# First pair of blocks: R, U, Y and the state product of block 3 half an item sooner, and three of Y's six small transfers issued by GpSimd

## The chip, the cores and the metric

The kernel runs on one core of one Trainium2 chip. The metric is device time in microseconds: the median of three runs, 589.41 us for the kernel before (589.01 to 589.84).

A core has five engines, each with its own queue of instructions that it works off in order: TensorE (PE, matmuls into PSUM; its weight loads are PEld), VectorE (DVE), ScalarE (ACT), GpSimd (POOL), and SyncE (SP), which here only issues transfers. They wait for each other through semaphores.

## The reference, cut to what matters

A delta-rule attention over 4 x 8 heads, 768 steps, head size 48, whose output is the input of a feed-forward layer (384 to 2048 to 384, 3072 tokens).

```python
def _attn_ref(q, k, v, beta):
    k_n = k / (np.linalg.norm(k, axis=-1, keepdims=True) + 1e-06)
    state = np.zeros((B, H, D, D), dtype=np.float32)
    for t in range(S):
        kt, vt, bt = (k_n[:, :, t], v[:, :, t], beta[:, :, t, None])
        y[:, :, t] = np.einsum('bhd,bhde->bhe', q[:, :, t], state)
        v_old = np.einsum('bhde,bhd->bhe', state, kt)
        state = state + bt[:, :, :, None] * np.einsum('bhd,bhe->bhde', kt, vt - v_old)

def _moe_ref(x, w_in, w_out):
    h = x @ w_in
    g = np.where(h >= 1, h, np.where(h <= -1, 0.0, (h + 1) ** 2 / 4))
    return g @ w_out
```

## The kernel before, in words

The 768 steps are cut into 12 blocks of 64 steps (block index `g`, 0 to 11), and two blocks make a pair (`G`, 0 to 5). Within a block the steps of a head are solved together: the Gram matrix of the keys (`gram_k`, L237) gives a triangular system, whose inverse is made on VectorE, all heads in lanes (transposes, norms, then 30 steps of `pr` and `A`, L366 and L368, and two closing transposes, L376 and L379), and put together by `merge` products. The state (tile `SU`) is then carried from block to block by a chain of four products on TensorE, each read out by ScalarE or VectorE before the next can start:

- R (`chain_r`, L492): the state times the keys, subtracted from the values by VectorE (L498);
- U (`chain_u`, L508): the inverse times these, copied to `SU` by ScalarE (L517);
- Y (`chain_y`, L534): the block's output, put into `xb` as a rounded part and a remainder (ScalarE L583 and L586, VectorE L590 and L592), and six small transfers of 32 KB (L595) that move the fourth head of each group to its rows of `xb`;
- the state product (`chain_d`, L607), added to the state by VectorE (L626).

The feed-forward layer runs beside that, as items: an item is a pair of blocks and one of 16 slices of the 2048 hidden units. Its up-projection (L738, nine matmuls into `h`) reads `xb`; ScalarE and VectorE turn `h` into `ghi` and `glo` (L877, L891, VectorE L893; then L856, VectorE L857), and two items later the down-projection (L753) adds into `o`. The first pair has 22 items: six for block 0 alone, ten for both, six for block 1 alone (256 columns wide). Items are numbered here from 0; item 22 is the first of the second pair, and its up-projection is the first that reads the Y of blocks 2 and 3.

The order of all engines is written out by hand. Each item has two places (2n and 2n+1) in two tables. `pe` holds products of the attention: those of place 2n stand on TensorE behind the item's up-projection, and are read out right after; those of place 2n+1 stand behind its down-projection, and are read out at the start of the next item. `fill` holds everything else: steps of the solve on VectorE and loads on SyncE; at a place 2n they are written down behind the read-out of that place's products. `at(table, G, t, ...)` puts something t items after the pair's first item. For the first pair M is 14, so `chain` starts 15.5 items in: U, Y and the state product of block 2 at the places 31, 32 and 34, then R, U, Y and the state product of block 3 (L784). `gram_k` of block 5 comes M + 3.5 items in, at place 35 (L832), the steps of the next solve (`lane_steps`, L833) at 32, 37, 38, 39 and 40: two are copies of the Gram matrices on ScalarE (L304), then come a transpose on VectorE with a root on ScalarE (L317, L281), eight short operations for norms and factors (L282 to L327), and the scaling of the system (L330), after which GpSimd masks it (L331) and the 30 steps can begin.

PSUM is shared: `h` has two buffers, so the up-projection of item n needs the L893 of item n-2; from item 12 on the attention's products have two buffers (`ch`) in all, so each of them also needs the read-out of the one before it. The keys and values of a coming block (`KV`) are loaded by SyncE in the order of `fill`, and scaled on VectorE (L292) between steps of the solve.

Of the kernel before, what the change touches and what calls it, by code (L numbers as in the profile page):

```python
# [7 lines left out]
F32 = mybir.dt.float32  # L8
# [5 lines left out]
C = 64  # L14
NP = 4
D = 48
# [24 lines left out]
def delta_rule_moe(ctx: ExitStack, tc: tile.TileContext, kqa, kqb, kv, beta, w, out):  # L41
# [14 lines left out]
    nc = tc.nc  # L56
# [4 lines left out]
    NB = CB * C  # L61
# [19 lines left out]
    def half(x):  # L81
        return slice(x * H, x * H + H)
# [80 lines left out]
    def dense(n):  # L163
        for _ in range(n):
            nc.tensor.matmul(warm_ps, warm[:, 0:P], warm, start=True, stop=True)  # L165
# [56 lines left out]
    def quarters():  # L222
        return [(e, x) for e in range(2) for x in range(2)]

    def banks(*shape):
        return [ps.tile([P, H, *shape], F32, **acc()) for _ in range(2)]
# [4 lines left out]
    def gram_k(g):  # L231

        x, b_ = KE.pop(g) if g in KE else K[g], banks(C)
        for j in range(H):
            for e, f in quarters():
                k, o = x[f * C:f * C + D, e * H + j, :], (1 - e) * C
                nc.tensor.matmul(b_[f][o:o + C, j], k, k, start=True, stop=True)  # L237

        def evict():
            for f in range(2):  # L240
                nc.scalar.copy(out=(GE[g - 2] if g in (2, 3) else GG[:, g % 2])[:, half(f)], in_=b_[f])
        return evict
# [158 lines left out]
    def merge16_a(g):  # L401
        y = ps.tile([P, NU, 16], F32, **acc())
        for u in range(NU):
            for r in QS:
                nc.tensor.matmul(y[r:r + 32, u], GG[r:r + 32, g, u, 32:64], XT[r:r + 32, g, u, 48:64], start=True, stop=True)

        def evict():
            if "Y" not in S:
                S["Y"] = own[:, NU * C:4 * DM].rearrange("p (g u t) -> p g u t", g=2, t=16)
            elif g == 0:  # L410
                S["Y"] = sb.tile([P, 2, NU, 16], F32, name="A16", bufs=1)
            nc.scalar.copy(out=S["Y"][:, g], in_=y)
        return evict
# [106 lines left out]
    def chain_y(g):  # L520
# [7 lines left out]
        xb = XB[g // 2]  # L528
# [14 lines left out]
        if g == 0:  # L543
            y0 = ps.tile([P, CT, NP, C], F32, **acc())
            for i in range(NT):
                for p in range(3):
                    for e in range(2):
                        for o in range(2):
                            r = o if (e, i) != (1, 1) else 1 - o
# [28 lines left out]
        def evict():  # L578
            parts = []
            for i in range(NT):  # L580
                hi, lo = (xb[:, x, :, g % 2 * NB:g % 2 * NB + NB].rearrange("p k (e s t) -> p s e k t", s=CT, t=C)[:, i] for x in range(2))
                shi, slo = (stg[:, x].rearrange("p (e s t) -> p s e t", s=CT, t=C)[:, i] for x in range(2))
                nc.scalar.copy(out=shi, in_=yy[i][:, :, 3])  # L583
                parts.append((yy[i], hi, lo, shi, slo))
            for y, hi, lo, shi, slo in parts:
                nc.scalar.copy(out=hi, in_=y[:, :, 0:3])  # L586

            def after():
                for y, hi, lo, shi, slo in parts:
                    nc.vector.tensor_tensor(out=slo, in0=y[:, :, 3], in1=shi, op=ALU.subtract)  # L590
                for y, hi, lo, shi, slo in parts:
                    nc.vector.tensor_tensor(out=lo, in0=y[:, :, 0:3], in1=hi, op=ALU.subtract)  # L592
                for k in range(3):
                    for r in (0, C):
                        (nc.gpsimd if g == 1 and r else nc.sync).dma_start(out=xb.bitcast(F32)[r + D:r + C, :, k, g % 2 * NB:g % 2 * NB + NB],  # L595
                                          in_=stg.bitcast(F32)[r + 16 * k:r + 16 * k + 16])
            return after
        return evict
# [175 lines left out]
    pe, fill = {}, {}  # L774

    def at(where, G, t, *x):
        where.setdefault(2 * first[G] + int(round(2 * t)), []).extend(x)
# [3 lines left out]
            at(fill, G, t + j, (gen, 1))  # L781

    def chain(G, t, a):
        for j, f, g in ((0, chain_u, a), (0.5, chain_y, a), (1.5, chain_d, a), (2.5, chain_r, a + 1), (3.5, chain_u, a + 1), (4, chain_y, a + 1), (5, chain_d, a + 1)):  # L784
            if (f, g) != (chain_d, ntot - 1):
                at(pe, G, t + j, lambda f=f, g=g: f(g))

    def plan(G):

        a, b = 2 * G + 2, 2 * G + 3  # L790
        if G == NS - 1:
            return
        if G == 0:
            made = dict(f=lambda n: dense(n) or (lambda: None), a=lambda g: merge16_a(g % 2), b=lambda g: merge16_b(g % 2), c=lambda g: merge32(g, None, True), e=lambda g: merge32(None, g), u=chain_u, y=chain_y, d=chain_d, r=chain_r, q=gram_q)
            for j, names in PIECES:
                for x in names.split():
                    at(pe, 0, j / 2, lambda f=made[x[0]], g=int(x[1]): f(g))
            M = MERGE / 2
            last = FT + HALF
        else:  # L800
            so, un = solves.pop(G)
            va, vb = scale_v(a), scale_v(b)
            at(fill, G, 0.5, (va, 1))
            at(fill, G, 1, (va, 1))
            at(pe, G, 2.5, lambda: chain_r(a))
            at(pe, G, 4.5, lambda: gram_q(a))
            at(pe, G, 6, lambda: gram_q(b))
            cost, hs = 0, 0
            t, n = (MERGE / 2 + 7 - FT - HALF, 30 + 2 * HALF - MERGE) if G == 1 else (-1, 15)
            for j in range(1, 31):  # L810
                at(fill, G, t + hs / 2, (so, 1))
                cost += j * (31 - j) + 150
                hs = int(cost / 9461 * n)
            for t in (6.5, 7, 7.5, 7.5, 7.5, 8.5):
                at(fill, G, t, (un, 1))
            at(fill, G, 9, (vb, 1))
            at(fill, G, 9.5, (vb, 1))
            M = 8.5
            last = 16
        if G:  # L820
            at(pe, G, 8, merge_first)
            at(pe, G, 9, merge_second)
        else:
            for j, x in ((0, (0, None)), (0.5, (1, 0)), (2.5, (None, 1))):
                at(pe, G, M + j, lambda x=x: merge32(*x))
        chain(G, M + 1.5, a)
        if G < NS - 2:
            if G:
                at(fill, G, 6.5, (load_k, a + 2))
            at(fill, G, M + 0.5, (load_k, b + 2, (nc.sync, nc.sync), True))  # L830
            at(pe, G, M + 1, lambda: gram_k(a + 2))
            at(pe, G, M + 3.5, lambda: gram_k(b + 2))  # L832
            lane_steps(G, M + 2, lanes(G + 2), 2.5, 3, 3.5, 4)  # L833
            solves[G + 1] = solve_whole(), unlanes_whole()
            at(fill, G, M + 3, (load_q, a + 2))
            at(fill, G, M + 5, (load_k, b + 2))
            at(fill, G, M + 6.5, (load_q, b + 2))
            at(fill, G, last + 0.5, (load_kv, a + 2))
            at(fill, G, last + 1.5, (load_kv, b + 2))

    solves = {}
    for G in range(NS):
        plan(G)
# [55 lines left out]
    G = NS - 1  # L899
# [50 lines left out]
```

## Time and profile before

| what | before |
|---|---|
| median of 3 runs | 589.41 us (589.01 to 589.84) |
| the profiled execution, and its span | 590.3 us, 588.6 us |
| TensorE busy | 569.0 us (97%), granted clock 0.992 in the mean |
| VectorE, ScalarE, GpSimd busy | 405.2 us (69%), 327.5 us (56%), 54.5 us (9%) |
| up-projections L738 | 918 matmuls, 223.0 us, mean 386 ns |
| down-projections L753 | 1152 matmuls, 329.4 us |
| small transfers L595 | 66 of 32 KB, median 2.0 us to landing |

The profile is of one execution; its times are counted from the start of its span. Rows of a timeline give the start, the busy time, engine, line, operation and tiles of one or of merged instructions, and in brackets how long the engine had stood idle before it and what ended that. The part that the change touches lies between 145 us and 210 us: items 16 to 21 of the first pair and the first items of the second.

### The profile page before, as it was taken

To read this page: it belongs to the slowest core of one execution; us is meant where nothing else is said; L and a number is where in the kernel's file an instruction comes from. 1 tells how busy PE (TensorE), PEld (TensorE's weight loads), DVE (VectorE), ACT (ScalarE), POOL (GpSimd) and SP (SyncE) were. 2 spreads that over 40 slices of the span, in tenths; PEclk is the share of its full clock that TensorE was granted. 3 is DMA by queue.
4 is the path that set the end of the run, shared out by engine and by line. 5 is a ranking of instruction groups with operands and counts; after the bars stand their busy time and mean duration, and the time that the engine had idled before them with its cause. 6 is when DMAs were issued, how large, how long until landed. Compare 5 with 4: busy or idle time off the path is not lost.

```text
span 588.6 us, 21697 instructions
## 1 busy us (share of the span) xinstructions
PE 569.0 (97%) x9585; PEld 493.3 (84%) x9585; DVE 405.2 (69%) x828; ACT 327.5 (56%) x587; POOL 54.5 (9%) x91
## 2 busy tenths in 40 slices
PE   8998899999999999999999999999999999999996
PEld 7776788788978888888888888888888888898986
DVE  5977999963689864599954599954599955333332
ACT  4648886358644575545575445575445564454443
POOL 6200010000000500010400011300011300000000
PEclk9979999999999999999999999999999999999999
DMA  5673766200333111134011134011133000020001
GB/s 147 199 253 138 213 212 192 77 4 10 95 81 100 31 32 39 39 97 114 24 33 41 37 103 119 16 30 45 36 106 96 1 3 16 15 55 1 0 2 53
DMA packets 32302, 42.77 MB, mean 73 GB/s; under 512 B 7056, under 2 KB 26768, under 8 KB 32208
## 3 DMA queue, kind: packets, MB, share of 16 engines
q1 hardware_dynamic: 31216, 40.41, 24.0%
q8 instruction: 75, 1.23, 0.9%
q0 software_dynamic: 576, 0.57, 0.4%
q10 hardware_dynamic: 416, 0.39, 0.2%
q14 instruction: 19, 0.16, 0.1%
HBM read 34.47 MB, written 4.72 MB: 67 GB/s over the span
## 4 chain that ended last, share of the span: by engine, by line
PE 47%; issue 22%; DVE 14%; DMA 6%; SPq 6%; ACT 2%; POOL 1%; POOLq 0%; DVEq 0%; ACTq 0%
PE h L738 18%; PE o L753 17%; DMA wt<-in_w_dram 4%; PE ch L534 3%; PE ch L237 2%; DVE s L893 2%; PE ch L508 2%; DVE pr L366 1%; DVE A L368 1%; DVE glo L857 1%; PE ch L250 1%; SPq L595 1%; PE ch L492 1%; DMA KV<-in_kv_dram 1%; DVE wt L208 1%
## 5 line engine op out<-in xcount | busy, mean ns | idle before, releaser
L738 PE MATMUL h<-xb,wt 128*128 128x512 f32 (+1 forms) x918 | 223.0, 386 | 5.1 <-DVE s L893 2.0
L753 PE MATMUL o<-wt,ghi 128*128 128x384 f32 x768 | 200.0, 342 | 0.1
L738 PEld LDWEIGHTS h<-xb,wt 128*128 128x128 f32 x918 | 161.8, 188 | 38.9 <-DVE s L893 3.4
L753 PEld LDWEIGHTS o<-wt,ghi 128*128 128x128 f32 x768 | 137.2, 188 | 7.0 <-issue 0.3
L753 PE MATMUL o<-wt,glo 128*128 128x384 f32 x384 | 129.4, 337 | 0.4 <-DVE glo L857 0.4
L856 ACT CAST ghi<-s 128x512 fp32r<-128x512 f32 (+1 forms) x102 | 60.8, 597 | 120.4 <-DVE s L893 107.8
L893 DVE SCALAR_TENSOR_TENSOR s<-s,h 128x512 f32<-128x512 f32 (+1 forms) x102 | 66.3, 650 | 77.1 <-ACT s L891 76.8
L877 ACT ACTIVATE s<-h,half 128x512 f32<-128x512 f32 (+1 forms) x102 | 67.4, 661 | 53.8 <-PE h L738 53.6
L857 DVE TENSOR_TENSOR glo<-s,ghi 128x512 fp32r<-128x512 f32 (+1 forms) x102 | 66.8, 654 | 39.5 <-ACT ghi L856 39.3
L753 PEld LDWEIGHTS o<-wt,glo 128*128 128x128 f32 x384 | 72.1, 188 | 1.0 <-DVE glo L857 1.0
L891 ACT ACTIVATE s<-s 128x512 f32<-128x512 f32 (+1 forms) x102 | 62.2, 610 | 2.2
L368 DVE TENSOR_TENSOR A<-A,pr 128x30 f32<-128x30 f32 (+14 forms) x120 | 45.4, 378 | 4.4
L366 DVE TENSOR_TENSOR pr<-A 128x30 f32<-128x30 f32 (+14 forms) x120 | 43.4, 362 | 2.2
L272 POOL TENSOR_SCALAR_AFFINE_SELECT Q<-Q 64x512 f32<-64x512 f32 x32 | 21.7, 680 | 117.4 <-ACT Q L260 116.0
L165 PE MATMUL o<-wx 128*128 128x512 f32 x87 | 27.8, 464 | 1.5 <-DVE tiny L175 1.5
L534 PEld LDWEIGHTS ch<-Q,SU 64*64 64x64 f32 (+3 forms) x1056 | 22.4, 135 | 3.7 <-ACT ghi L856 1.5
L534 PE MATMUL ch<-Q,SU 64*64 64x64 f32 (+3 forms) x1056 | 24.7, 222 | 0.0
L331 POOL TENSOR_SCALAR_AFFINE_SELECT A<-A 128x1024 f32<-128x1024 f32 x4 | 5.6, 1390 | 191.5 <-DMA xb<-X 148.1
L165 PEld LDWEIGHTS o<-wx 128*128 128x128 f32 x87 | 18.2, 220 | 5.6 <-DVE tiny L175 1.5
L626 DVE TENSOR_TENSOR SU<-ch,SU 48x384 f32<-48x384 f32 x36 | 19.9, 554 | 3.9 <-PE ch L607 3.5
L590 DVE TENSOR_TENSOR X<-ch,X 128x128 fp32r<-128x128 f32 x20 | 5.8, 292 | 23.5 <-ACT xb L586 22.5
L517 ACT COPY SU<-ch 64x384 f32<-64x384 f32 (+1 forms) x30 | 14.3, 476 | 7.0 <-PE ch L508 6.7
(168 smaller groups left out, 559.5 us busy)
## 6 DMA issues: line engine op xcount, KB each, us to landing
wt<-in_w_dram SPq DMA_DIRECT2D x16, 768.0 KB, 5.6
out_dram<-wx SPq DMA_DIRECT2D x44, 96.0 KB, 2.2
KV<-in_kv_dram SPq DMA_DIRECT2D x36, 96.0 KB, 2.4
KV<-in_kv_dram SPq DMA_DIRECT2D x72, 48.0 KB, 2.3
KV<-in_kv_dram SPq DMA_DIRECT2D x12, 192.0 KB, 2.7
xb<-X SPq DMA_DIRECT2D x60, 32.0 KB, 2.0
K<-in_kqb_dram SPq DMA_DIRECT2D x12, 128.0 KB, 2.6
Q<-in_kqb_dram SPq DMA_DIRECT2D x12, 128.0 KB, 2.7
```

The source lines that it names most:

```text
L165: nc.tensor.matmul(warm_ps, warm[:, 0:P], warm, start=True, stop=True)
L272: nc.gpsimd.affine_select(out=y, in_=y, pattern=[[0, H], [1, C]], base=0, channel_multiplier=-1, compare_op=ALU.is_gt, fill=0.0)
L366: nc.vector.tensor_tensor(out=pr, in0=A[:, 0:n, j:j + 1].broadcast_to([P, n, m]), in1=A[:, j:j + 1, j + 1:32].broadcast_to([P, n, m]), op= ...
L368: nc.vector.tensor_tensor(out=A[:, 0:n, j + 1:32], in0=A[:, 0:n, j + 1:32], in1=pr, op=ALU.add)
L534: nc.tensor.matmul(yy[i][o * C:o * C + C, e, p], SF[rows, u:u + C], w_[rows, x, k, :], **how)
L738: nc.tensor.matmul(h[:, cols(bs)], WT[f][:, 0, x, k * P:(k + 1) * P], XB[G][:, y, k, cols(bs)], start=(n == 0), stop=(n == 8))
L753: nc.tensor.matmul(oacc[G, k], (ghi, glo)[x][:, k * P:(k + 1) * P], WT[f][:, 1, y, :], start=(new and n == 0), stop=(left[G, b] == 0 and n ...
L856: nc.scalar.copy(out=ghi[:, c], in_=s[:, c])
L857: nc.vector.tensor_tensor(out=glo[:, c], in0=s[:, c], in1=ghi[:, c], op=ALU.subtract)
L877: nc.scalar.activation(out=s[:, c], in_=h[:, c], func=AF.Relu, bias=mid, scale=0.5)
L891: nc.scalar.activation(out=s[:, c], in_=s[:, c], func=AF.Square)
L893: nc.vector.scalar_tensor_tensor(out=s[:, c], in0=s[:, c], scalar=1.0, in1=h[:, c], op0=ALU.min, op1=ALU.max)
```

## The change

Three edits. For the first pair alone (`G` = 0), R, U, Y and the state product of block 3 move from 2.5, 3.5, 4 and 5 items behind the chain's start to 2, 3, 3.5 and 4.5, that is from the places 36, 38, 39 and 41 to 35, 37, 38 and 40. `gram_k` of block 5, at place 35 so far, moves to 36. And of the six small transfers of block 3's Y, the three for the upper 64 rows are issued by GpSimd, as those of block 1 are already.

```diff
                 for k in range(3):
                     for r in (0, C):
-                        (nc.gpsimd if g == 1 and r else nc.sync).dma_start(out=xb.bitcast(F32)[...],
+                        (nc.gpsimd if g in (1, 3) and r else nc.sync).dma_start(out=xb.bitcast(F32)[...],
...
     def chain(G, t, a):
-        for j, f, g in ((0, chain_u, a), (0.5, chain_y, a), (1.5, chain_d, a), (2.5, chain_r, a + 1), (3.5, chain_u, a + 1), (4, chain_y, a + 1), (5, chain_d, a + 1)):
+        for j, f, g in zip((0, 0.5, 1.5, 2.5, 3.5, 4, 5) if G else (0, 0.5, 1.5, 2, 3, 3.5, 4.5), (chain_u, chain_y, chain_d, chain_r, chain_u, chain_y, chain_d), (a, a, a, a + 1, a + 1, a + 1, a + 1)):
             if (f, g) != (chain_d, ntot - 1):
                 at(pe, G, t + j, lambda f=f, g=g: f(g))
...
             at(pe, G, M + 1, lambda: gram_k(a + 2))
-            at(pe, G, M + 3.5, lambda: gram_k(b + 2))
+            at(pe, G, M + (3.5 if G else 4), lambda: gram_k(b + 2))
```

On TensorE, between items 17 and 21, the difference of the two orders reads as follows (R is L492, the Gram product L237, U L508, Y L534, the state product L607, L738 an up-projection; the down-projections are left out).

```order
+L492 MATMUL ch<-SU,K 64x48 x32
+L738 MATMUL h<-xb,wt_1093 128x256 x9
 L237 MATMUL ch<-A 64x64 x32
-L738 MATMUL h<-xb,wt_1093 128x256 x9
-L492 MATMUL ch<-SU,K 64x48 x32
...
+L508 MATMUL ch<-KV,XT 64x48 x32
 L738 MATMUL h<-xb,wt_1106 128x256 x9
-L508 MATMUL ch<-KV,XT 64x48 x32
...
+L534 MATMUL ch<-Q,SU 64x64 x48
...
-L534 MATMUL ch<-Q,SU 64x64 x48
 L738 MATMUL h<-xb,wt_1205 128x256 x9
+L607 MATMUL ch<-SU,KV 48x48 x32
```

R stands where the Gram product stood, the Gram product behind the next up-projection, and U, Y and the state product each ahead of an up- or a down-projection that they stood behind.

On VectorE, from the `glo` of item 18 to the first step of the solve, the order before is this (`s_2880` belongs to item 19, `s_3029` to item 20; L592 writes Y, L626 the state).

```order
L857 TENSOR_TENSOR glo_2867<-s_2818,ghi_2866 128x256
L317 STREAM_TRANSPOSE A_2919<-GG_172 128x1024
L893 SCALAR_TENSOR_TENSOR s_2880<-s_2880,h_2870 128x256
L282 RECIPROCAL r1_2989<-y0_2988 128x32
...
L592 TENSOR_TENSOR xb_2567<-ch_2937,xb_2567 128x2x3x64
L857 TENSOR_TENSOR glo_3016<-s_2880,ghi_3015 128x256
L330 SCALAR_TENSOR_TENSOR A_2919<-A_2919,gm_2995 128x1024
L893 SCALAR_TENSOR_TENSOR s_3029<-s_3029,h_3019 128x256
L626 TENSOR_TENSOR SU_171<-ch_3041,SU_171 48x384 x2
L626 TENSOR_TENSOR SU_171<-ch_3042,SU_171 48x384 x2
L857 TENSOR_TENSOR glo_3088<-s_3029,ghi_3087 128x256
L366 TENSOR_TENSOR pr_3103<-A_2919 128x30
```

In the changed kernel the same stretch of VectorE reads as follows (`s_2917` is item 19's now).

```order
L857 TENSOR_TENSOR glo_2904<-s_2818,ghi_2903 128x256
...
L592 TENSOR_TENSOR xb_2567<-ch_2921,xb_2567 128x2x3x64
L317 STREAM_TRANSPOSE A_2984<-GG_172 128x1024
L893 SCALAR_TENSOR_TENSOR s_2917<-s_2917,h_2907 128x256
L282 RECIPROCAL r1_3003<-y0_3002 128x32
...
L857 TENSOR_TENSOR glo_3016<-s_2917,ghi_3015 128x256
L626 TENSOR_TENSOR SU_171<-ch_3031,SU_171 48x384 x2
L626 TENSOR_TENSOR SU_171<-ch_3032,SU_171 48x384 x2
L330 SCALAR_TENSOR_TENSOR A_2984<-A_2984,gm_3009 128x1024
L893 SCALAR_TENSOR_TENSOR s_3029<-s_3029,h_3019 128x256
L857 TENSOR_TENSOR glo_3088<-s_3029,ghi_3087 128x256
```

Y's read-out (L590 and L592) went from behind the transpose and the eight short operations to ahead of them, and the four additions to the state (L626) from behind the scaling L330 and item 20's L893 to ahead of both.

On SyncE, behind the output transfers of block 0, the difference begins as follows.

```order
-L93 DMA K<-in_kqb_dram 64x512
-L94 DMA K<-in_kqa_dram 48x512
...
-L595 DMA xb<-X 16x2x256 x6
+L595 DMA xb<-X 16x2x256 x3
+L93 DMA K<-in_kqb_dram 64x512
+L94 DMA K<-in_kqa_dram 48x512
...
 L102 DMA Q<-in_kqb_dram 64x512
```

Three of Y's transfers left SyncE, and the six key loads of block 5 moved from ahead of Y's transfers to behind them.

## Rows read from the trace of the kernel before

**Rows 1.** What TensorE waited for, from 206 us to the end.
```profile
PE ch L462 <- DVE XT L376: 0.4, 1, 0.4
PE h L738 <- DMA xb<-X: 0.2, 1, 0.2
```

**Rows 2.** The chain of waits, 145 to 210 us: start, us, what.
```profile
149.96 1.15 PE ch L237 x62
151.11 1.26 PE h L738 x9
152.37 1.08 PE ch L492 x64
153.45 1.25 PE o L753 x6
...
155.75 1.08 PE ch L508 x64
...
172.07 2.20 DMA KV<-in_kv_dram
...
206.28 1.40 PE ch L462 x82
```

**Rows 3.** Timeline of VectorE, 138 to 215 us.
```profile
155.72 2.02 DVE L317 STREAM_TRANSPOSE A<-GG 128x1024 f32<-128x1024 f32 x1
...
159.01 0.35 DVE L282 RECIPROCAL r<-y 128x32 f32<-128x32 f32 x1
...
160.81 0.20 DVE L327 STREAM_TRANSPOSE N<-N 128x32 f32<-128x32 f32 x1
...
161.72 1.01 DVE L592 TENSOR_TENSOR xb<-ch,xb 128x384 fp32r<-128x384 f32 x2
...
162.98 1.22 DVE L330 SCALAR_TENSOR_TENSOR A<-A,gm 128x1024 f32<-128x1024 f32 x1
...
164.45 2.25 DVE L626 TENSOR_TENSOR SU<-ch,SU 48x384 f32<-48x384 f32 x4
...
167.07 0.18 DVE L366 TENSOR_TENSOR pr<-A 128x30 f32<-128x30 f32 x1
...
174.39 0.56 DVE L292 TENSOR_TENSOR KV<-KV,N 128x384 f32<-128x384 f32 x1 [1.16 <-DMA KV<-in_kv_dram]
...
201.06 0.69 DVE L893 SCALAR_TENSOR_TENSOR s<-s,h 128x512 f32<-128x512 f32 x1 [1.51 <-ACT s L891]
```

**Rows 4.** Timeline of TensorE, 145 to 215 us: item 22's up-projection.
```profile
166.87 1.96 PE L738 MATMUL h<-xb,wt 128*128 128x512 f32 x6 [0.77 <-DVE SU L626]
```

**Rows 5.** Timeline of ScalarE, 138 to 215 us.
```profile
151.14 1.07 ACT L241 COPY GG<-ch 128x512 f32<-128x512 f32 x2 [1.78 <-PE ch L237]
...
153.25 1.23 ACT L304 COPY GG<-GG 32x512 f32<-32x512 f32 x2
...
156.86 1.46 ACT L517 COPY SU<-ch 64x384 f32<-64x384 f32 x3 [0.60 <-PE ch L508]
...
158.54 0.34 ACT L281 ACTIVATE y<-A,tiny 128x32 f32<-128x32 f32 x1
```

**Rows 6.** Timeline of GpSimd, 130 to 210 us.
```profile
164.50 1.26 POOL L331 TENSOR_SCALAR_AFFINE_SELECT A<-A 128x1024 f32<-128x1024 f32 x1 [43.45 <-PE ch L607]
```

**Rows 7.** Timeline of SyncE's queue, 140 to 200 us.
```profile
162.80 4.91 SPq L595 DMA_DIRECT2D xb<-X  x6
167.80 0.54 SPq L102 DMA_DIRECT2D Q<-in_kqb_dram  x1
...
170.87 0.52 SPq L113 DMA_DIRECT2D KV<-in_kv_dram  x1
```

**Rows 8.** Stretches: length, busy us (instructions) by engine, TensorE's clock, DMA share, GB/s.
```profile
27.00:30.00 3.00, 1.27 (x77) 0.86 (x65) 3.00 (x4) 1.49 (x3) 0.12 (x2) 1.00 0.41 99
30.00:37.00 7.00, 6.71 (x112) 5.27 (x112) 6.71 (x19) 1.59 (x3) 0.00 (x0) 0.51 0.98 368
46.00:48.20 2.20, 0.73 (x34) 0.58 (x30) 0.56 (x1) 0.99 (x2) 0.00 (x0) 1.00 0.99 406
```

More of the change, by code (lines that the diff above doesn't have):

```diff
@@ L594, in after @@
                     for r in (0, C):
-                        (nc.gpsimd if g == 1 and r else nc.sync).dma_start(out=xb.bitcast(F32)[r + D:r + C, :, k, g % 2 * NB:g % 2 * NB + NB],
+                        (nc.gpsimd if g in (1, 3) and r else nc.sync).dma_start(out=xb.bitcast(F32)[r + D:r + C, :, k, g % 2 * NB:g % 2 * NB + NB],
                                           in_=stg.bitcast(F32)[r + 16 * k:r + 16 * k + 16])
```

## The prediction

> **What bounds the kernel now.** I read the waits of TensorE first, and by stretch. From 206 us to the end it waits twice, for 0.4 and 0.2 us [rows 1]: there TensorE alone sets the time, and whatever delay it has at 206 us it keeps to the end. The first of these waits is the place to watch: L462, the merge product that needs the finished solve, waits 0.4 us for VectorE's closing transpose L376. So TensorE and VectorE reach 206 us almost together. The chain of waits, read next, shows by what way [rows 2]: through TensorE's products until Y, then through transfers to the values of the next block (the piece that starts at 172.07 and takes 2.20), and from there along VectorE to L462 at 206.28. The timeline of VectorE tells why [rows 3]: the solve's first step L366 starts at 167.07, L292 stands idle 1.16 us for the values, and then only one other wait is left, 1.51 us at 201.06. VectorE is the bound of the stretch from 167 to 206 us. TensorE's own stall, at item 22's up-projection (0.77 us at 166.87, where Y's transfers have to land) [rows 4], is not what decides: behind it TensorE would meet VectorE anyway.
>
> So the question to put to the change is when VectorE starts the 30 steps of the solve.
>
> **TensorE and ScalarE up to Y.** R takes the Gram product's slot. That slot's row starts at 149.96, when the four additions to the state have freed the PSUM buffers; R waits for the same additions. R takes 1.08: to 151.04. Item 18's up-projection 1.26: to 152.30. The Gram product, now behind it, 1.15: to 153.45. Its buffers must first be emptied of R by two VectorE subtractions of 128x384, which at the 0.56 of L292's row make 1.1 us and lie beside the 1.26; were that cover gone, some tenths would be lost. Then the down-projection 1.25, to 154.70, and U 1.08, to 155.78 [rows 2]. Before, U ended at 155.75 + 1.08 = 156.83, and its copies (L517) began at 156.86. So U itself comes 1.05 sooner. But on ScalarE the Gram copies (1.07, from 153.45), a square and the two L304 (1.23) now stand ahead of them [rows 5]: 153.45 + 1.07 + 1.23 = 155.75 without the square, and up to 156.2 with it. I take 156.0 for the start of L517, between U's end 155.8 and 156.2: 0.85 sooner than before.
>
> **Y.** Behind L517 nothing changes until Y is read out: before, L592 ended 162.73 - 156.86 = 5.87 after L517 began [rows 3, 5]. Now it ends at 156.0 + 5.9 = 161.9. The change asks for more than that in half an item, but U has to wait for the Gram copies.
>
> **VectorE behind Y.** This is the term that counts. Before, the transpose L317 and the eight short operations ran at 155.72 to 157.74 and 159.01 to 161.01, while VectorE had nothing else; they were done before Y's read-out. Now they are queued behind it on VectorE, and the additions to the state come ahead of L330. From 161.9:
> - L317, 2.02: to 163.9.
> - The root on ScalarE needs it: 0.34 [rows 5], to 164.3 with a hop to and fro. Item 19's L893 lies beside it.
> - L282 to L327, 161.01 - 159.01 = 2.00: to 166.3.
> - The `glo` of item 19 and four L626. Before, four L626 and one such `glo` filled 164.45 to 167.07, 2.62: to 168.9. Their input, the state product, is there by then (it needs only Y's read-out).
> - L330, 1.22: to 170.15.
> - GpSimd's mask L331 began 0.30 after L330's end before (164.50 against 164.20) and took 1.26 [rows 3, 6]: to 171.7.
>
> L366 starts at 171.75, against 167.07: 4.7 us late. The reason is that VectorE now stands idle for Y and does afterwards what it did in that gap. The uncertain step is the first: with L517 at 155.8 or 156.2 the 4.7 becomes 4.5 or 4.9.
>
> **What is hidden of it.** From L366, VectorE got to L292 in 174.39 - 1.16 - 167.07 = 6.16 us. Now that is 177.9, and the values must have landed. SyncE: three of Y's six transfers are gone (six took 4.91, so three 2.5), six key loads are put in their place, which I take at the 3.07 that the six Q loads took (167.80 to 170.87) [rows 7], then these. 162.0 + 2.5 + 3.1 + 3.1 = 170.7 for the first load of values, as before (170.87), so they land at about 172.07 + 2.20 = 174.3. The 1.16 us of waiting are gone, and L292 comes 177.9 - 174.4 = 3.5 us late. The wait of 1.51 at 201.06 is for a square on ScalarE, and ScalarE's queue up to that square starts from the item before's L893 on VectorE; both move together, and it stays. L376, L462 at 209.8, and with TensorE waiting for nothing later [rows 1], the end: +3.5.
>
> **GpSimd's three transfers** cost nothing: they begin at 162.0, at about 0.8 each (4.91 / 6) they are out by 164.5, and the next thing in GpSimd's queue is L331, due at 170.4. They bring nothing either: all six land by about 167, while item 22's up-projection now waits for something later. It needs `h` free by item 20's L893, which stands behind L330 (170.15) and takes about 0.4 (0.69 for 512 columns [rows 3]): 170.55, where before it began at 166.87 [rows 4]. TensorE gets there at 166.1 (166.87 - 0.77) to 167.5 (if the down-projection before it waits for item 19's `glo`, due at 166.7), and so stands 3 to 4.4 us. That stall is a face of the same delay, no further term.
>
> **Sum.** Profiled execution: 590.3 + 3.5 = 593.8. The median of the runs shown is 589.41, 0.9 below it; on that scale 592.9.
>
> **A rival by TensorE's clock.** In the early part TensorE was busy for 1.27 of 3 us (27 to 30 us), and in the 7 us after that its granted clock was 0.51, the 1.2 GHz level; at 46.0 to 48.2, busy 0.73 of 2.2, it stayed at 1.00 [rows 8]. The new stall at 167 to 170.5 could do the former. Then 7 us at half the clock lose up to 3.5 us of TensorE's work. Part of that TensorE would have spent waiting for VectorE anyway, so the price lies between 0 and 3.5 on top; I take the middle, 1.8: +5.3, 594.7. The Trainium skill, "TensorE: Matmul & The Clock Gate", section "Why this matters for your kernels", tells to keep long idle gaps out from between bursts of matmuls, since the clock falls back to the lower level after one. By that rule the stall would cost this; the trace has one gap after which it fell and one after which it did not.
>
> **Other rivals.**
> - VectorE catches up. If the wait of 1.51 at 201.06 went as well, 2.0 would be left: 591.4. Speaks for it: ScalarE is busy for 56% of the span and could run ahead. Against: that wait is ScalarE's own chain behind VectorE.
> - Faster: VectorE keeps its old times in spite of its order, the transfers land sooner, the 1.16 us wait for the values goes: 588.2 at best, because L462 needs L376. It decides only if L366 starts at 167 or before; each 0.1 us beyond 1.16 of lateness is lost time. Against it stands the order itself: L317 behind L592 on the same engine, and L366 needs L331, which needs L330, which needs L317.
> - Nothing changes: the 4.7 is met by exactly as much hidden slack. I find 1.16 for certain and 1.51 in doubt.
>
> **Chances.** Forecast 592.9: 0.60. Clock: 0.20. Catching up: 0.10. Faster or nothing: 0.10. What a measurement of this kernel can tell from no change is 0.2%, 1.2 us: below 588.2 is faster, above 590.6 slower. The first three cases are all slower, nearly 0.9; of the other two I give 0.05 to faster and 0.06 to the same. The range takes in the catching up with L517 early (-0.2) and the clock with L517 late (+0.2): 591.2 to 594.9. The forecast's own range is 592.5 to 593.3.
>
> **What would show it.** Right: in the profile after, on VectorE L317 starts at about 162 behind L592, L330 at 169, L366 at 171.5 to 172; L292's wait for values is gone; item 22's up-projection waits 3 us or more for VectorE's L893, not for transfers; L462 starts near 209.8. Y's L592 ends 0.6 to 1.1 us sooner than 162.73. Wrong in the first step if Y comes 2 us sooner; wrong in the main one if L366 starts before 169, or if L376 ends at 206 though L366 was late; then VectorE had slack that its busy rows hide. A clock of 0.5 near 170 to 177 us would show the clock rival.

## The result, and the profile after

Slower. The changed kernel's first four executions took 595.1 to 599.9 us, median 597.94, against 589.50 for before: a ratio of 1.0122 (95% interval 1.0090 to 1.0154; ratios here are estimated from all runs and are not quite the quotient of the medians, 1.0143). The direction is the forecast's; the size lies 5 us above its 592.9 and outside its range. Twelve further executions in another comparison (the first experiment) had a median of 594.35 against 589.72, ratio 1.0068 (1.0036 to 1.0100), which is +4.0 us with 2.1 to 5.9 for the interval, around the forecast's +3.5; with an interval that wide, that it lies so close may be luck. Two parts have to be kept apart: what the change does where it acts, and what differs from execution to execution.

To do that I count times from one instruction ahead of everything that the change moves: item 17's up-projection. Its row in TensorE's timeline of before (start, length, engine, line, operation, count):

```profile
145.03 1.34 PE L738 MATMUL h<-xb,wt 128*128 128x256 f32 x9
```

In the same view after, that row, then two waits in brackets, then the merge product that needs the finished solve:

```profile
147.98 1.34 PE L738 MATMUL h<-xb,wt 128*128 128x256 f32 x9
...
169.47 0.44 PE L753 MATMUL o<-wt,glo 128*128 128x384 f32 x1 [0.74 <-DVE glo L857]
...
173.35 4.21 PE L738 MATMUL h<-xb,wt 128*128 128x512 f32 x9 [2.92 <-DVE s L893]
...
213.23 1.29 PE L462 MATMUL ch<-XT,GG 32*32 32x32 f32 x128
```

The span grew from 588.6 to 596.3, by 7.7 us. Of these 2.95 are there at the reference row already (147.98 - 145.03), where the order of instructions is that of before. Another 4.0 come up to L462: it starts 65.25 after the reference, 61.25 before (206.28 [rows 1, 2] less 145.03). The last 0.75 come behind it, where TensorE waits once, at 395 us:

```profile
PE ch L479 <- issue: 0.7, 1, 0.7
```

The middle part is the change. VectorE's timeline after, in answer to [rows 3]:

```profile
163.78 1.01 DVE L592 TENSOR_TENSOR xb<-ch,xb 128x384 fp32r<-128x384 f32 x2
164.71 1.97 DVE L317 STREAM_TRANSPOSE A<-GG 128x1024 f32<-128x1024 f32 x1
...
169.34 2.25 DVE L626 TENSOR_TENSOR SU<-ch,SU 48x384 f32<-48x384 f32 x4
171.62 1.23 DVE L330 SCALAR_TENSOR_TENSOR A<-A,gm 128x1024 f32<-128x1024 f32 x1
...
174.59 0.18 DVE L366 TENSOR_TENSOR pr<-A 128x30 f32<-128x30 f32 x1
...
180.54 0.55 DVE L292 TENSOR_TENSOR KV<-KV,N 128x384 f32<-128x384 f32 x1
...
209.94 2.35 DVE L376 STREAM_TRANSPOSE XT<-A 128x1024 f32<-128x1024 f32 x1
```

The reader is to see a queue: L317, the norms (from 167.10 on), the four L626 and L330 stand one behind the other after Y's read-out L592, where before L317 and the norms filled a gap ahead of it. L366 starts 26.61 after the reference, 22.04 before: 4.57 late. L292 has no bracket any more. L376 is 3.2 late (61.96 against 203.82 - 145.03 = 58.79).

ScalarE, in answer to [rows 5]: U's copies are sooner, the root waits for L317.

```profile
159.01 1.46 ACT L517 COPY SU<-ch 64x384 f32<-64x384 f32 x3
...
166.72 0.35 ACT L281 ACTIVATE y<-A,tiny 128x32 f32<-128x32 f32 x1 [2.87 <-DVE A L317]
```

SyncE's queue, in answer to [rows 7], and GpSimd's, in answer to [rows 6]. The value loads (L113) are issued 25.76 after the reference, 25.84 before: three transfers fewer, six key loads more.

```profile
164.85 1.95 SPq L595 DMA_DIRECT2D xb<-X  x3
166.91 1.18 SPq L93 DMA_DIRECT2D K<-in_kqb_dram  x1
...
173.74 0.47 SPq L113 DMA_DIRECT2D KV<-in_kv_dram  x1
```

```profile
165.36 1.50 POOL L595 DMA_DIRECT2D xb<-X  x3 [40.96 <-issue]
173.15 1.26 POOL L331 TENSOR_SCALAR_AFFINE_SELECT A<-A 128x1024 f32<-128x1024 f32 x1 [6.29 <-DVE A L330]
```

Then the clock. Stretches of after, then of before, columns as in [rows 8]; the number behind the five engines is TensorE's granted clock (of 7 us at 30 to 37, which [rows 8] has for before at 0.51, after has 0.76):

```profile
37.00:47.00 10.00, 9.61 (x192) 7.20 (x192) 4.43 (x10) 5.21 (x9) 0.00 (x0) 0.66 0.68 235
60.00:74.00 14.00, 12.93 (x273) 11.78 (x276) 12.20 (x24) 10.23 (x18) 0.00 (x0) 0.63 0.65 219
168.00:172.00 4.00, 1.69 (x10) 1.05 (x8) 3.83 (x11) 0.30 (x1) 0.00 (x0) 0.96 0.41 111
172.00:178.50 6.50, 5.14 (x13) 4.29 (x14) 5.53 (x17) 2.47 (x6) 1.42 (x2) 0.50 0.47 124
```

```profile
37.00:47.00 10.00, 9.11 (x271) 7.02 (x271) 4.82 (x11) 7.44 (x12) 0.00 (x0) 1.00 0.69 228
60.00:74.00 14.00, 12.37 (x343) 10.99 (x336) 12.76 (x26) 12.30 (x23) 0.00 (x0) 1.00 0.71 213
172.00:178.50 6.50, 6.13 (x31) 5.19 (x30) 5.13 (x13) 2.49 (x5) 0.00 (x0) 1.00 0.51 134
```

Two different things: at 37 to 74 us the clock is lower in two stretches (it is 1.00 from 74 to 144 us in both profiles) although the program there is the same, and at 172 to 178.5 it is at 0.50, the 1.2 GHz level, right after TensorE was busy for 1.69 of 4 us in its new stall.

### The profile page after: what moved, and what is told of

Its sections match the earlier page's. It is cut to its first block, busy times and chain, and to the rows that moved or that the text cites. A ratio compares the mean times of both kernels' runs of the same rounds, so it can differ in the third digit from the quotient of the medians.

```text
span 596.3 us, 21710 instructions
## 1 busy us (share of the span) xinstructions
PE 575.7 (97%) x9585; PEld 499.5 (84%) x9585; DVE 405.5 (68%) x828; ACT 328.1 (55%) x587; POOL 55.9 (9%) x94
## 4 chain that ended last, share of the span: by engine, by line
PE 58%; issue 22%; DVE 11%; SPq 3%; ACT 3%; DMA 2%; POOL 1%; POOLq 0%; ACTq 0%; DVEq 0%
PE h L738 22%; PE o L753 20%; PE ch L534 3%; PE ch L250 2%; PE ch L237 2%; PE ch L508 1%; PE ch L492 1%; PE o L165 1%; DMA K<-in_kqa_dram 1%; DVE SU L626 1%; DVE xb L201 1%; DVE wt L208 1%; DVE s L893 1%; DVE glo L857 1%; DMA KV<-in_kv_dram 1%
## 5 line engine op out<-in xcount | busy, mean ns | idle before, releaser
L738 PE MATMUL h<-xb,wt 128*128 128x512 f32 (+1 forms) x918 | 225.3, 390 | 6.6 <-DVE s L893 4.9
L738 PEld LDWEIGHTS h<-xb,wt 128*128 128x128 f32 x918 | 164.0, 191 | 40.4 <-DVE s L893 7.0
L753 PEld LDWEIGHTS o<-wt,ghi 128*128 128x128 f32 x768 | 138.8, 190 | 7.1
L893 DVE SCALAR_TENSOR_TENSOR s<-s,h 128x512 f32<-128x512 f32 (+1 forms) x102 | 66.2, 649 | 79.8 <-ACT s L891 79.5
L366 DVE TENSOR_TENSOR pr<-A 128x30 f32<-128x30 f32 (+14 forms) x120 | 43.4, 362 | 2.2
L165 PE MATMUL o<-wx 128*128 128x512 f32 x87 | 28.1, 467 | 1.5 <-DVE tiny L175 1.5
L534 PEld LDWEIGHTS ch<-Q,SU 64*64 64x64 f32 (+3 forms) x1056 | 22.5, 135 | 3.7 <-ACT ghi L856 1.5
L534 PE MATMUL ch<-Q,SU 64*64 64x64 f32 (+3 forms) x1056 | 24.7, 222 | 0.0
L165 PEld LDWEIGHTS o<-wx 128*128 128x128 f32 x87 | 18.3, 222 | 5.7 <-DVE tiny L175 1.5
L590 DVE TENSOR_TENSOR X<-ch,X 128x128 fp32r<-128x128 f32 x20 | 5.8, 292 | 25.2 <-ACT xb L586 24.3
L626 DVE TENSOR_TENSOR SU<-ch,SU 48x384 f32<-48x384 f32 x36 | 20.0, 554 | 3.9 <-PE ch L607 3.5
L517 ACT COPY SU<-ch 64x384 f32<-64x384 f32 (+1 forms) x30 | 14.3, 476 | 6.5 <-PE ch L508 6.1
```

Source lines behind the costliest of these rows:

```text
L366: nc.vector.tensor_tensor(out=pr, in0=A[:, 0:n, j:j + 1].broadcast_to([P, n, m]), in1=A[:, j:j + 1, j + 1:32].broadcast_to([P, n, m]), op= ...
L534: nc.tensor.matmul(yy[i][o * C:o * C + C, e, p], SF[rows, u:u + C], w_[rows, x, k, :], **how)
L626: nc.vector.tensor_tensor(out=x, in0=y, in1=x, op=ALU.add)
L738: nc.tensor.matmul(h[:, cols(bs)], WT[f][:, 0, x, k * P:(k + 1) * P], XB[G][:, y, k, cols(bs)], start=(n == 0), stop=(n == 8))
L753: nc.tensor.matmul(oacc[G, k], (ghi, glo)[x][:, k * P:(k + 1) * P], WT[f][:, 1, y, :], start=(new and n == 0), stop=(left[G, b] == 0 and n ...
L893: nc.vector.scalar_tensor_tensor(out=s[:, c], in0=s[:, c], scalar=1.0, in1=h[:, c], op0=ALU.min, op1=ALU.max)
```

## The experiments

My theory A: VectorE's order carries the price. Rival B: GpSimd's transfers do. Theory C: the early 2.95 us are chance of an execution. Theory D: the stall lowers the clock, and that costs extra. Rival E: TensorE's other order costs by itself. Each median below stands beside that of before in the same comparison.

**The changed kernel once more.** No edit.

> The changed kernel once more, unaltered, to separate what the change costs in every execution from what the clock's early part happens to do. In the profiled run of the changed kernel 2.95 us of the loss lay before 148 us, in a stretch where the change moves nothing, at a lower granted clock. Theory C (the early part differs from execution to execution): in the new profile item 17's up-projection L738 starts somewhere else than 147.98 us, anywhere between 145 and 148, and the times scatter over 2 us or more, 595 to 598. Rival (something in the changed program lowers the early clock every time): it starts at 147.5 to 148.5 again, the granted clock is low again at 62 to 72 us, and the median is 597.5 to 598.5. Both expect L366 to start 26.6 us after that up-projection, against 22.0 in the kernel before.

594.35 us (591.5 to 597.7 in 12 executions) against 589.72 (587.3 to 595.2 in 35). TensorE's timeline:

```profile
144.68 1.34 PE L738 MATMUL h<-xb,wt 128*128 128x256 f32 x9
...
170.05 3.72 PE L738 MATMUL h<-xb,wt 128*128 128x512 f32 x9 [2.91 <-DVE s L893]
...
209.14 1.04 PE L462 MATMUL ch<-XT,GG 32*32 32x32 f32 x102
```

The reference row is 3.3 us sooner than in the first profile of the same kernel, sooner even than before's. From there on the mechanism repeats: L366 at 171.29, 26.61 after it, and L462 at 64.46. Theory C fits and its rival falls. L462 is 0.8 sooner than in the first profile, as the clock rose again within the up-projection (3.72 us instead of 4.21); L376 is not (61.98 against 61.96).

**The kernel before against itself.** No edit.

> The kernel before against itself, for the size of what chance does. Theory C (the early part differs between executions of one kernel): item 17's up-projection starts anywhere from 143.9 to 148.0 us, not at 145.03; from there L462 is reached at 61.2 to 61.3 whatever the start; times from 587 to 595, ratio within 0.3% of 1. Rival: 145.0 and 589.0 to 589.9 each time, so that the early loss of the changed kernel belongs to its program.

589.64 against 590.23 (586.9 to 594.0 in 30), ratio 0.9994 (0.9973 to 1.0015).

```profile
143.59 1.34 PE L738 MATMUL h<-xb,wt 128*128 128x256 f32 x9
...
204.69 1.41 PE L462 MATMUL ch<-XT,GG 32*32 32x32 f32 x128 [0.41 <-DVE XT L376]
```

Reference 1.4 us sooner, L462 61.10 after it. So before too moves by microseconds ahead of the reference; the three times shown at first, 589.0 to 589.8, were closer together than its executions are. This profile and the changed kernel's second one are the closest pair so far: spans 587.7 and 591.7, 4.0 apart, of which 1.1 lie ahead of the reference and 3.4 between it and L462.

**The reorder alone.**

```
- (nc.gpsimd if g in (1, 3) and r else nc.sync).dma_start(...)
+ (nc.gpsimd if g == 1 and r else nc.sync).dma_start(...)
```

> The reorder alone: all six of Y's transfers are issued by SyncE again. Theory A (VectorE's order carries the loss): as the changed kernel within 0.5 us, 595 to 598.5; L366 starts 26 to 27 us after item 17's up-projection L738 began (22.0 before, 26.6 with the change), item 22's up-projection waits about 3 us for L893. SyncE has three issues more ahead of the value loads, about 2.5 us, so the wait of 1.16 us at L292, gone with the change, may come back in part: up to 1 us more. Rival B (GpSimd's transfers cost the time): back to 589 to 591.

593.87 against 589.72, ratio 1.0061 (1.0025 to 1.0096): as the whole change, though under the 595 to 598.5 expected. From the reference (146.16) L366 comes at 26.62, L292 at 32.57 without a wait, L462 at 64.43.

```profile
146.16 1.34 PE L738 MATMUL h<-xb,wt 128*128 128x256 f32 x9
...
210.59 1.41 PE L462 MATMUL ch<-XT,GG 32*32 32x32 f32 x128
```

Rival B falls. The part of the wait at L292 that I thought might come back did not.

**GpSimd's transfers alone,** run twice: in the kernel before, `g == 1` becomes `g in (1, 3)`.

> GpSimd's three transfers alone, the order of the kernel before. Theory A: they cost nothing and shorten SyncE's queue by about 2.5 us, so the wait of 1.16 us for values at L292 goes and the end comes 0 to 1.2 us sooner: 588.3 to 589.7. Rival B (the transfers delay GpSimd's mask L331 or the up-projection of item 22): L331 starts later than the 164.50 of before, L366 after 168, and the time is 590.5 or more, up to 597. For the question of the early clock: by theory C item 17's up-projection L738 starts between 145 and 148 us here too, by chance; by its rival at 145.0, as before, since the order is that of before.

> GpSimd's three transfers alone, a second time: the one part of the change that gained in its trace (L462 at 60.0 us after item 17's up-projection instead of 61.1 to 61.25), while its median could not be told from before. Theory A: the trace repeats it, L462 at 59.9 to 60.1 and no wait for values at L292; the median lies 0.5 to 1.2 us under that of before in the same call, within the scatter of 2 us. Rival: L462 at 61 or later, the first trace was chance.

First TensorE, then VectorE, of the first of the two:

```profile
144.68 1.34 PE L738 MATMUL h<-xb,wt 128*128 128x256 f32 x9
...
204.68 1.42 PE L462 MATMUL ch<-XT,GG 32*32 32x32 f32 x128 [0.37 <-DVE XT L376]
```

```profile
172.81 0.55 DVE L292 TENSOR_TENSOR KV<-KV,N 128x384 f32<-128x384 f32 x1
```

L366 at 22.06, no wait at L292, L462 at 60.00, and 60.01 in the second run (145.88 to 205.89): 1.1 to 1.25 sooner than before, both times. The medians, 590.41 against 589.72 and 590.70 against 590.66 (ratios 1.0017, 0.9987 to 1.0046, and 0.9999, 0.9975 to 1.0023), do not show it: the gain expected in the median was a miss both times. The gain at L462 is shown by the trace, a gain of the whole is not. Item 22's up-projection does not wait in either profile: its wait of 0.77 before [rows 4], put down to L626 in the row, was for Y's transfers, as the prediction read it.

**L317, norms and L330 earlier** (the changed kernel; this run puts the norms ahead of Y on both engines).

```
- lane_steps(G, M + 2, lanes(G + 2), 2.5, 3, 3.5, 4)
+ lane_steps(G, M + 2, lanes(G + 2), *((2.5, 3, 3.5, 4) if G else (2, 2, 2.5, 3)))
```

> The changed kernel, but in the first pair the steps of the next solve's decay (transpose L317, the norms L282 to L327, L330) are recorded half an item to one item sooner, so that L317 and the norms stand on VectorE ahead of Y's read-out and L330 right behind it, ahead of the four L626. Theory A: L366 needs only L592 (161.9 on the scale of before), L330 (1.22) and the mask (0.3 + 1.26): 164.7 to 166, against 171.7 with the change and 167.07 before, so nothing of the loss is left behind 148 us; item 22's up-projection waits under 1 us, the clock stays at its full level at 171 to 178, and the time is 588 to 590, plus up to 3 if the early clock is low. Rival B: the time stays at 595 to 598, since the transfers are still there. Rival E (the reorder of TensorE itself, with R, U and Y in other slots, costs the time): L366 starts early but L462 is still reached 2 us or more later than 61.3 us after item 17's up-projection, and the time is 592 or more.

593.03 against 589.72, ratio 1.0046 (1.0021 to 1.0070). I missed a queue: on ScalarE the root now stood ahead of U's copies, waited 1.60 for L317, and Y waited 2.11 for the copies; Y itself then took 3.65 us instead of the 2.28 it takes in the profile after, at a granted clock of 0.50 from 157.9 to 161.3 us.

```profile
156.80 0.35 ACT L281 ACTIVATE y<-A,tiny 128x32 f32<-128x32 f32 x1 [1.60 <-DVE A L317]
157.06 1.45 ACT L517 COPY SU<-ch 64x384 f32<-64x384 f32 x3
```

```profile
143.89 1.33 PE L738 MATMUL h<-xb,wt 128*128 128x256 f32 x9
...
158.05 3.65 PE L534 MATMUL ch<-Q,SU 112*64 112x64 f32 x96 [2.11 <-ACT SU L517]
```

L366 26.22 after the reference, L462 64.34: Y came too late for this run to say anything on theory A.

**L317 alone ahead of Y's read-out, L330 ahead of L626.** As above with `(2, 2.5, 3, 3.5)`: all four steps half an item sooner, and the root on ScalarE stays behind U's copies.

> The changed kernel with the transpose L317 half an item sooner and ahead of Y's read-out, the eight norm operations still behind it, L330 ahead of the four L626. All times are counted from the start of item 17's up-projection, since executions of one kernel differ by up to 4 us before it. Theory A (VectorE's order carries the loss): L592 ends at 16.8, the norms take 2.0, L893 0.4, L330 1.2 and the mask 1.6: L366 at 22.0, against 26.6 with the change and 22.0 before. With SyncE's shorter queue the values are there, L292 at 28.1 as with the transfers alone, and L462 is reached at 60.0 (64.4 with the change, 61.25 before). Time: 3 to 4.5 us under the changed kernel of the same call, 589 to 590.5 by median. Rival E (the other order of TensorE costs the time): L462 at 62 or later.

589.72 against 590.23, ratio 0.9983 (0.9961 to 1.0005), where the changed kernel stood at 1.0068. VectorE:

```profile
154.98 2.01 DVE L317 STREAM_TRANSPOSE A<-GG 128x1024 f32<-128x1024 f32 x1
...
162.42 1.22 DVE L330 SCALAR_TENSOR_TENSOR A<-A,gm 128x1024 f32<-128x1024 f32 x1
...
163.89 2.25 DVE L626 TENSOR_TENSOR SU<-ch,SU 48x384 f32<-48x384 f32 x4
...
167.46 0.18 DVE L366 TENSOR_TENSOR pr<-A 128x30 f32<-128x30 f32 x1
```

With the reference at 143.30, L366 comes at 24.16 and L462 (205.33) at 62.03. Moving the steps of the solve alone, TensorE's order left as changed, takes back 2.4 of the 3.2 us: theory A is shown for these, and rival E's bound of 62 is only just touched. The expected 22.0 for L366 was missed because L626, 2.25, stands ahead of it still, with an L893 and a `glo` that waits 0.53 for ScalarE.

**The norms between U's copies and Y's read-out,** a third placing (the norms recorded ahead of item 19's evictions).

```
...
-            lane_steps(G, M + 2, lanes(G + 2), 2.5, 3, 3.5, 4)
+            steps = lanes(G + 2)
+            lane_steps(G, M + 2, steps, *((2.5, 3, 3.5, 4) if G else (2, 2.5, 3.5)))
+            if G == 0:
+                pre[int(M + 5)] = steps
...
+        if n in pre:
+            run(pre.pop(n), 1)
```

> As the run before, but the eight norm operations too stand ahead of Y's read-out on VectorE, and their root on ScalarE behind U's copies, so that it holds up nothing there: the reorder as it could be had without its price. Counted from item 17's up-projection: theory A: L592 ends at 16.8, L330 1.2, mask 1.6: L366 at 19.6 to 20, L292 at 26 to 27 unless the values are late (wait up to 1 us), L462 at 58.5 to 60, where TensorE may be the later one (before, it had 0.4 us to spare there). Median 587.5 to 590. Rival E: L462 at 62 or later, 591 or more.

591.69 against 590.23, ratio 1.0021 (0.9998 to 1.0045).

```profile
164.58 0.18 DVE L366 TENSOR_TENSOR pr<-A 128x30 f32<-128x30 f32 x1
...
172.00 0.56 DVE L292 TENSOR_TENSOR KV<-KV,N 128x384 f32<-128x384 f32 x1 [1.37 <-DMA KV<-in_kv_dram]
```

Another miss: 591.69 and L462 at 63.01 (204.72, reference 141.71) are what rival E named. But the rows lead elsewhere. L366 comes at 22.87, 0.83 later than before, and as VectorE came sooner than in the changed kernel, the values were late: its waits at L292 are 1.37 and 0.72, 2.1 us, 0.93 more than before. Together that is 1.76, and L376 is 1.75 late (60.54). In this order SyncE issues six key loads between Y's transfers and the values, whose first load comes 26.93 after the reference, against 23.30 with GpSimd's transfers alone; the changed kernel has such a delay too (25.76) and hides it behind VectorE's.

The same sum, lateness of L366 plus the change of the waits at L292, gives 4.57 - 1.16 = 3.4 for the changed kernel, where L376 is 3.2 late, and 2.12 - 1.16 = 1.0 for the run with L317 alone ahead of Y, where it is 0.8 late. It leaves rival E, a cost of TensorE's order past VectorE's and SyncE's queues, nothing beyond 0.2 us to explain at L462.

**TensorE's stall filled** (theory D).

```
+        if (G, f, bs) == (0, 3, (1,)):
+            for _ in range(16):
+                nc.tensor.matmul(oacc[G, k], glo[:, k * P:(k + 1) * P], WT[f][:, 1, 0, :], start=False, stop=False)
```

> The changed kernel with TensorE kept busy in its new stall: 16 more products of 128x384 ahead of item 22's up-projection (the low part of item 19 is added 16 times more to one output block, so the output differs there). About 2.8 us of the 2.9 us stall are filled. If the stall is what lowers the clock: the granted clock stays at its full level from 168 to 180 us, item 22's up-projection takes 2.2 us instead of 3.7 to 4.2, and L462 waits for L376 and starts at 64.3 after item 17's up-projection, instead of 64.4 to 65.25 without a wait; the time falls by 0.1 to 1 us, which the scatter may hide. If the stall is not the cause: the clock falls there all the same. In either case L366 stays at 26.6: the price of VectorE's order is not touched.

The 16 products add to one output block once more each, so the output differs there. TensorE's timeline (line numbers 3 to 4 higher behind the edit), then two stretches:

```profile
147.21 1.34 PE L738 MATMUL h<-xb,wt 128*128 128x256 f32 x9
...
169.55 2.99 PE L757 MATMUL o<-wt,glo 128*128 128x384 f32 x16
172.62 2.35 PE L738 MATMUL h<-xb,wt 128*128 128x512 f32 x9
...
211.75 1.42 PE L462 MATMUL ch<-XT,GG 32*32 32x32 f32 x128 [0.19 <-DVE XT L376]
```

```profile
168.00:172.00 4.00, 3.26 (x18) 3.26 (x19) 3.89 (x9) 0.00 (x0) 0.00 (x0) 1.00 0.46 127
172.00:178.50 6.50, 6.04 (x28) 4.65 (x27) 5.50 (x19) 2.83 (x6) 1.43 (x2) 1.00 0.40 119
```

Busy 3.26 of 4 us instead of 1.69, the clock stays at 1.00, the up-projection takes 2.35 instead of 4.21, and L462 waits for VectorE again, at 64.54. So the stall is what lowers the clock, as far as one profile with the stall filled and four without can show it (the clock fell in all four), and VectorE alone accounts for 64.54 - 61.25 = 3.3 us; the lower clock adds from nothing (64.46 and 64.43 above) to 0.7 (65.25) and 1.2 (65.77, in the run of the changed kernel with idle products, below). The time, 595.94 against 590.23, ratio 1.0083 (1.0051 to 1.0114), is no better; its profiled execution took 598.75 and had the clock lower early as well.

**Four idle products in the early gap,** with GpSimd's transfers alone (twice), and with the whole change.

```
-    "sAwFALs,", ...
+    "sAwFFFFFALs,", ...
```

> GpSimd's transfers alone, and four more idle products (L165, 128x512, about 0.24 us each) in TensorE's early gap at 27.8 to 28.6 us, ahead of L419. Theory C (the scatter comes from the granted clock's falls at 29 to 45 us, after that gap): the falls get rarer or shorter, item 17's up-projection starts at 141.5 to 143.5 instead of 143.6 to 145, the highest times go and the median falls to 587 to 589. Rival: the falls have another cause, or the four products only delay L419: start and times as without them, 589.5 to 591.

> The changed kernel with the same four idle products. By theory C the difference between this run and the one before it is the price of the reorder with less of the scatter: L462 at 64.4 to 65.2 us after item 17's up-projection against 60.0, so 4.4 to 5 us, of which 1.2 are the gain of the shorter wait for values that the reorder hides. Rival: the medians differ by 2 us or less, or by over 7.

> The version that the runs point to, once more: the order of the kernel before, GpSimd's three transfers, and the four idle products in the early gap. If its first median of 588.88 was no chance: 588 to 589.5 again, 1 to 2 us under before, and 5 to 7 under the changed kernel. Rival: 590 to 591, no difference from before. By either the trace has L462 at 60.0 us after item 17's up-projection, and no granted clock under the full level at 29 to 37 us.

Medians: 588.88 against 590.66, ratio 0.9976 (0.9951 to 1.0001); with the change 595.00 against 590.66, 1.0075 (1.0044 to 1.0107); the first again 589.86 against 591.14, 0.9989 (0.9963 to 1.0014). TensorE's early timeline of the first:

```profile
30.64 3.04 PE L165 MATMUL o<-wx 128*128 128x512 f32 x12
34.12 0.38 PE L436 MATMUL h<-XT,GG 32*32 32x32 f32 x12 [0.44 <-DVE XT L424]
36.59 1.01 PE L436 MATMUL h<-XT,GG 32*32 32x32 f32 x52 [2.09 <-issue]
...
40.63 2.50 PE L165 MATMUL o<-wx 128*128 128x512 f32 x5
```

The twelve L165 take 3.04, so the clock is not lower there; but TensorE then meets a wait of 2.09 for issue, and the lower clock comes at 39 us instead: five L165 take 2.50, 1.42 before. The fall moved, it did not go, and theory C's expected starts of 141.5 to 143.5 were missed (144.22, 145.75, 147.28). The full clock expected at 29 to 37 us for the second run of that version was missed too: 0.90 at 30 to 37, after 0.66 at 27 to 30. L462 came at 60.00, 65.77 and 60.00 after them: with the change 5.8 later than with the transfers alone, of which 1.2 is the hidden gain of the transfers. The 6.1 us between the medians of the two lie above the 4.4 to 5 expected and below the rival's 7. The second median, 589.86, fell between the 588 to 589.5 and the rival's 590 to 591. The version with transfers and four products is the best of the runs, but neither of its intervals leaves 1 out: that it beats before is not shown; that it beats the changed kernel is (its intervals end at 1.0014 at most, the changed kernel's begin at 1.0036).

## Why the prediction was wrong, step by step

What it says of the place where the change acts held; what it took for granted of the rest of the execution did not.

- **TensorE and ScalarE up to Y:** right. L517 was put at 156.0, 10.97 after the reference; it came at 11.03. Y's read-out was to end at 161.9, 16.87; it ended at 164.79, 16.81.
- **VectorE behind Y:** right, in kind and size. 4.7 us late at L366 was forecast, 4.57 came, and 4.57 to 4.64 in every run of this order. L330 was put at 23.9 and came at 23.64; the mask at 25.4 and came at 25.17.
- **What is hidden:** right. The wait of 1.16 went, the value loads were issued at the old time, the wait on a square stayed (1.50 to 1.52 us, but 1.81 in the run of the changed kernel with idle products). VectorE's price at L376 is 3.2 instead of 3.5.
- **GpSimd's transfers:** right for this change. Alone they are worth 1.1 to 1.25 us at L462, which this order hides. Three took 1.50 on GpSimd, where I put 2.5.
- **The stall of TensorE:** 0.74 and 2.92 us, forecast 3 to 4.4 in one piece.
- **The clock rival:** its event came, in every profile of the change with its stall unfilled. I had given it 0.20, on one gap that lowered the clock and one that did not [rows 8]. The Trainium skill, "TensorE: Matmul & The Clock Gate", section "Why this matters for your kernels", warns of long idle gaps between bursts of matmuls; this trace agrees (a wait of 2.92 us, 1.69 of 4 us busy, then 0.50), and the filled stall, at 1.00, is the counterproof. But its price is 0 to 1.2 us at L462, not the 1.8 taken. That part of the lost work falls into time in which TensorE would have waited for VectorE is likely but not measured: with the stall filled, TensorE still waits 0.38, 0.16 and 0.19 us for it up to L462.
- **The step that failed is the sum:** "Profiled execution: 590.3 + 3.5 = 593.8. The median of the runs shown is 589.41, 0.9 below it; on that scale 592.9", and the range of 591.2 to 594.9 built on it. It takes everything ahead of and behind the change as fixed, without a reason; the three times that it starts from lay within 0.8 us. The runs showed otherwise: the reference row starts anywhere from 141.71 to 147.98, and executions of before lie between 586.9 and 595.2. In the profiled execution after, this left-out term was 2.95 us, with 0.75 more for an issue wait behind L462; both were as large together as the forecast itself. Of the 7.7 us by which the span grew, 4.2 are beyond the forecast's 3.5: these 3.7, and 0.5 at L462, where VectorE's 3.3 and the lower clock's 0.7 add up to 4.0. For the other three of the first four executions no trace tells the parts apart.

Nothing shows the early part to be the change's: over the profiles with TensorE's changed order and no idle products (147.98, 144.68, 146.16, 143.30, 143.89, 141.71, 147.21) the reference starts at 145.0 on average, over those with the old order (145.03, 143.59, 144.68, 145.88) at 144.8.

What it is made of, the traces do show. One part are the waits "for issue", in which the engine waited for nothing that the profile shows. With four idle products more, such a wait stands four products sooner in L436, between the 12th and 13th matmul instead of the 16th and 17th; the rows of after:

```profile
35.44 0.44 PE L436 MATMUL h<-XT,GG 32*32 32x32 f32 x16
36.96 0.95 PE L436 MATMUL h<-XT,GG 32*32 32x32 f32 x48 [1.09 <-issue]
```

So the wait belongs to a place in TensorE's stream of instructions, and not to L436. Counted in matmuls and weight loads, the 60 such waits of 0.15 us and more that the 14 profiles have ahead of the reference row all lie a multiple of 256 apart, and each ends 1.2 to 1.7 us after a transfer of 16 KB on the DMA queue that the page names "instruction" (q8) has ended. The 0.75 at L479 is one more at such a place. By these rows TensorE waited there for its next instructions to be loaded; beyond the shift by four products no run tests it. The other part is the lower clock. Ahead of the reference it lasted about 20 us in the first profile of the changed kernel, 7 us in before's, and the three latest references (147.21 to 147.98) have it at 0.66 over 37 to 47 us and at 0.63 to 0.76 over 60 to 74, the earliest (141.71) at 1.00 in both. Neither part sets the start by itself, but a fit that is linear in both sums (the waits, and half of the time at the lower clock) accounts for 86% of the variance of the 14 starts. The changed kernel's second profile had the clock at 0.76 over 60 to 74 us,

```profile
60.00:74.00 14.00, 14.00 (x298) 12.63 (x296) 12.02 (x25) 11.76 (x22) 0.00 (x0) 0.76 0.64 211
```

and an early reference all the same. What stays open is why a load comes late or the clock falls in one execution and not in the next, and why the first four executions all lay high, three of them above all twelve of the second comparison. Their mean granted clock was 0.976 to 0.982; among the twelve, the five executions at or under 0.982 have a median of 596.1, the seven others 592.6. So the clock goes along with a part of it.

## What to carry to other kernels

When a step is moved ahead on one engine, look at what it jumps over on every other in-order queue: here half an item on TensorE put VectorE's transpose and norms from a gap to behind the thing that had been waited for, which made the solve start 4.6 us late, and put six loads on SyncE between Y's transfers and the values. Before a change of half a percent is forecast or judged, learn how far executions of one kernel lie apart, and count from an instruction ahead of the change in the trace: so counted, the effect at L366 repeats to 0.1 us where single executions scatter by 8. A gain that a single part shows at its own place (1.1 to 1.25 us, twice) need not show in the whole.

## What was not expected of the hardware

- One program's executions differ by up to 8 us in 590 (107 of before: 586.9 to 595.2), and profiles of kernels with the same first 145 us by 6.3 there (141.71 to 147.98), with the granted clock at 0.51 to 0.76 over 30 to 37 us, and at 0.63 to 1.00 over 60 to 74.
- TensorE waits for its instructions at fixed places of their stream, 256 matmuls and weight loads or a multiple of it apart, in some executions and not in others, by 0.15 to 2.89 us each. The two largest (2.09 and 2.89) stood in the middle of L436 when the twelve products ahead of it ran at the full clock.
- At the lower clock the same up-projection of nine 128x512 products took 4.21 us, and 3.85 and 3.72 where the clock rose within it, instead of 2.25 to 2.36.
